# A hand-written planner's DMA costs and the searched order of TensorE's units in a fused attention and feed-forward kernel

## The chip, the cores and the metric

One NeuronCore of one Trainium2 chip. The metric is device microseconds of one execution. Engines are written PE (TensorE), ACT (ScalarE), DVE (VectorE), POOL (GpSimd) and SP (SyncE); PEld is PE's weight load.

## The reference

Attention with "talking heads" (the heads are mixed before and after the softmax), then a feed-forward layer with a squared relu. Eight batches, 12 heads, 448 positions, head size 64, and 2048 hidden units.

```python
scores = scale * q @ k.T                              # [8, 12, 448, 448]
scores = einsum('bhij,hg->bgij', scores, w_pre)       # mix the heads
attn   = exp(scores - max); attn /= sum(attn) + 1e-9
attn   = einsum('bhij,hg->bgij', attn, w_post)        # mix them again
x      = (attn @ v) as [3584, 768]
out    = relu(x @ w_in) ** 2 @ w_out                  # [3584, 768], float32
```

## The kernel before

Matmuls are in bfloat16 and everything runs in one pass over the eight batches, whose stages overlap. Work is recorded as tasks; a task on PE is called a unit. For batches 1 to 7 the way of one batch is:

- **Load.** q, k and v come by DMA from POOL's queue (`load_qk`, `load_v`; L657, L668), the two weights too (`emit_load_w`, L693). DVE makes rounding copies of q and k (`qkr`, L751), PE transposes them (L760), and they are copied to `qkt`.
- **QK** (`emit_QK`, L903). The batch's 448 query rows are cut into four tiles (three of 128 rows, one of 64), written b_T here: 4_3 is tile 3 of batch 4. A unit does two or four heads; ACT or DVE copies each head's scores from PSUM to `stage` (L479 on ACT, L480 on DVE; these two lines serve all copies out of PSUM). `stage` has two slots, used by the tiles in turn.
- **Relayout** (`emit_rel`, L949). The head mix needs 10 query rows x 12 heads on the partitions. SP issues one DMA for every chunk of 10 rows, from `stage` to one of 16 slots of `dring`; chunks that lie across two tiles take two. A batch has 49. All wait for the copies of their tile, and SP issues them in order. The first copy of tile n into `stage` waits until all relayouts of tile n-2 have landed (`old`).
- **Pre-mix** (`emit_pre`, L972). One unit mixes two chunks; ACT takes the exponential and its row sums (`pring`, L989), DVE the reciprocals (L1003), POOL folds them into the weights of the second mix (L1010, L1025).
- **Post-mix** (`emit_post`, L1055 and L1070), which also transposes; its result is copied to `a2t`.
- **AV** (`emit_AV`, L1136) in two halves of a batch, to `xt`.
- **First layer** (`emit_F1`, L1215; L1187 for batches 0 and 1), relu on ACT or DVE (`h1t`), square on DVE (`h2t`).
- **Second layer** (`emit_F2`, L1332; L1281 at the end), copy to `osb`, and the output's DMA from POOL's queue.

Batch 0 does without relayouts for its first 240 rows (L833, L859).

PE's units use its array in five tilings (whole, two halves of rows, four quadrants and others); neighbours in the order may differ in it.

What sets the order is `_Plan`, which runs at build time and whose times never reach the chip. The units stand in ten streams (0 transposes, 1 QK, 2 pre-mix, 3 post-mix, 4 AV, 5 the mix of batch 0's first rows, 6 and 7 first layer, 8 and 9 second layer), and `ORDER` is a string of 947 digits: the next digit names the stream that gives PE's next unit. The string was found by a search against the planner's own times. Between the units `run` places all other tasks: of those that are ready it takes the one that can start first, and a copy or a relu goes to whichever of ACT and DVE would end it first by the planner's costs. So the planner's costs decide where each task stands in its engine's queue and on which engine it runs; on the chip each engine goes through its queue in order and waits on semaphores.

DMAs are of two kinds for the planner, "move" (relayouts) and "load" (all others). `dma_push` notes one when it is issued, with its work in ns; `dma_next` lets both kinds run beside each other at reduced rates and gives the end: the time at which the work is done, and `DMA_END` of its kind on top. SP's queue is held for 1050 ns by each relayout, 850 in batch 0.

Of the kernel before, what the change touches and what calls it, by code (L numbers as in the profile page):

```python
# [21 lines left out]
FETCH = (110e3, 6000.0, 4600.0, 1400.0)  # L22
DMA_START = {"move": 1420.0, "load": 1350.0}
DMA_AHEAD = 3900.0
DMA_END = {"move": 2800.0, "load": 2300.0}
INF = float("inf")
ORDER = (
    "0010000110000111100000000000000005555100511515000015555333555553335555302305155003331254"
    "2211441136332276223766133377223616731226633137114442227663367171613367762227767121623771"
    "3393329122990302183381228324442006627183100281118131813381227673216731326612236773372224"  # L30
    "4411361663177132200663221776338333811282282277006331767332672238001811183118322442293391"
    "3191319222911933392244224431911613362200721731632363732176221673273360021673372281008113"
    "8222891319113933192222443813811381338222444422363163371172261161373372200611637327220062"
    "1637337229300911191139222818323833182222444391139311913392224418223813422813811613622007"
    "3372263362173373262136733702062163711722009139311919222444223811383138111833822281444382"
    "2286116307137062236713733631672127622167337002283812288030911393119311922244422939113933"
    "1913822281183338122444222636371173622267137633363711761263722179228393398128383392224442"
    "2833876383786676767367222676783338444867667766767677679989998888999"
)


# [57 lines left out]
class _Plan:  # L99
# [96 lines left out]

    def dma_push(self, t, start):
        kind, work, packet = t.dma
        at = start + DMA_START[kind]
        if kind == "move" and at < 30e3:  # L200
            at += 600.0
        elif kind == "move" and not self.moving["move"]:
            behind = sum(x[1] for x in self.moving["load"] if x[0] <= at)
            at += min(DMA_AHEAD, max(0.0, behind - max(0.0, at - self.moved)))
        self.moving[kind].append([at, work, packet, t])

    def dma_next(self, go=False):
# [28 lines left out]
        if go:  # L236
            self.moved = now
            for i, y in enumerate((a, b)):
                if y is not None:
                    y[1] = left[i]  # L240
            t = x[3]
            self.moving[t.dma[0]].pop(0)
            t.end = max(t.end, now + DMA_END[t.dma[0]]
                        + (1800.0 if t.dma[0] == "load" and 20e3 < now < 45e3 else 0.0))
# [1251 lines left out]
```

## Time and profile before

| | |
|---|---|
| median of 3 runs | 537.45 us (536.75 to 537.5) |
| the profiled execution | 539.38 us, span 537.6 us |
| mean granted clock of PE | 0.990 |
| busy: PE, ACT, DVE, POOL | 508.3, 436.8, 404.9, 266.3 us |
| DMA | 72.03 MB |
| relayouts in the trace | 365 issues on SP, median 0.905 us each to issue |

Busy time is the time in which an engine has an instruction of its own under way; the rows of an engine's groups give the number of instructions, their mean length and the idle time just before them with what ended it. A granted clock of 1.00 is TensorE's full clock. The profiled execution includes 1.8 us outside the span.

### The profile page before, as it was taken

Reading aid. Unit: us, or ns where it says so; the run is one execution under the profiler, and the core shown is the slowest. Engines: PE = TensorE matmul, PEld = TensorE weight load, DVE = VectorE, ACT = ScalarE, POOL = GpSimd, SP = SyncE. Lnnn points to the kernel's source line nnn. Section 1 sums busy time; section 2 is a strip of 40 time slices with the busy share of each in tenths; the row PEclk is TensorE's granted clock in tenths of the full one; section 3 lists DMA queues with packets and bytes.
Section 4 is the critical chain, followed back from the end, with each engine's and each line's share of the span. In section 5 each row is a group of like instructions: output and inputs, shape, how many; then the busy total and the mean of one; then the engine's idle time right before and its main releaser. Section 6 shows DMA issues by size and latency. Waiting matters only on the chain.

```text
span 537.6 us, 22063 instructions
## 1 busy us (share of the span) xinstructions
PE 508.3 (95%) x8923; PEld 315.1 (59%) x8923; DVE 404.9 (75%) x1057; ACT 436.8 (81%) x1257; POOL 266.3 (50%) x571
## 2 busy tenths in 40 slices
PE   7899999898899996999979999899899999999997
PEld 3355775666666653567535665456545665568874
DVE  8799978688888686877869768887598777965440
ACT  4799999888899895888978999888788888876521
POOL 9926557335763484335733668225735436343100
PEclk9899999999999999999989999999999999999999
DMA  8999999647894689347984579536986668354004
GB/s 112 207 214 182 205 182 180 167 83 136 159 186 96 138 158 190 63 87 151 173 155 102 116 152 203 127 60 134 168 146 119 131 130 160 65 93 104 4 16 104
DMA packets 83065, 72.03 MB, mean 134 GB/s; under 512 B 7572, under 2 KB 80468, under 8 KB 82964
## 3 DMA queue, kind: packets, MB, share of 16 engines
q0 software_dynamic: 37632, 33.83, 39.3%
q1 hardware_dynamic: 45044, 36.59, 29.7%
q8 instruction: 72, 1.18, 0.9%
q14 instruction: 29, 0.24, 0.1%
q10 hardware_dynamic: 288, 0.20, 0.1%
HBM read 47.22 MB, written 11.01 MB: 108 GB/s over the span
## 4 chain that ended last, share of the span: by engine, by line
PE 65%; DMA 13%; ACT 11%; DVE 3%; POOL 3%; SPq 2%; issue 1%; DVEq 0%; ACTq 0%; POOLq 0%
PE ps L1332 22%; PE ps L1215 16%; DMA dring<-stage 8%; ACT pring L989 6%; PE ps L1136 5%; PE ps L972 5%; PE ps L903 4%; PE ps L1055 4%; DMA vraw<-in_v_dram 3%; ACT a2t L479 2%; PE ps L1187 2%; DMA kraw<-in_k_dram 2%; SPq L949 2%; PE ps L1281 2%; DVE stage L480 2%; ACT stage L479 1%
## 5 line engine op out<-in xcount | busy, mean ns | idle before, releaser
L989 ACT ACTIVATE pring<-ps 128x448 bf16<-128x448 f32 x360 | 191.3, 564 | 9.5 <-PE ps L972 8.6
L1332 PE MATMUL ps<-w_out_sb,h2t 64*128 64x384 bf16 x1664 | 151.3, 323 | 0.6 <-DVE a2t L480 0.2
L1010 POOL TENSOR_TENSOR wk2s<-wk2b,rinv 128x120 bf16<-128x120 bf16 (+1 forms) x179 | 70.7, 395 | 162.7 <-DVE rinv L1003 161.5
L480 DVE CAST a2t<-ps 128x420 bf16<-128x420 f32 (+1 forms) x200 | 120.4, 638 | 14.2 <-PE ps L1070 13.5
L480 DVE CAST stage<-ps 128x448 bf16<-128x448 f32 (+1 forms) x182 | 109.3, 616 | 27.3 <-DMA dring<-stage 14.2
L1215 PE MATMUL ps<-xt,w_in_sb 64*128 64x448 bf16 (+2 forms) x1344 | 124.3, 327 | 3.9 <-DVE stage L480 3.6
L479 ACT ACTIVATE stage<-ps 128x448 bf16<-128x448 f32 (+1 forms) x178 | 92.2, 556 | 29.7 <-PE ps L903 15.8
L479 ACT ACTIVATE a2t<-ps 128x420 bf16<-128x420 f32 (+1 forms) x168 | 100.5, 659 | 12.5 <-PE ps L1070 12.3
L1332 PEld LDWEIGHTS ps<-w_out_sb,h2t 64*128 64x128 bf16 x1664 | 76.9, 94 | 51.3 <-issue 2.5
L1215 PEld LDWEIGHTS ps<-xt,w_in_sb 64*128 64x128 bf16 x1344 | 61.7, 95 | 45.1 <-DVE stage L480 3.1
L989 ACT ACTIVATION_READ_ACCUMULATOR pring<-ps 128x1 f32 x360 | 82.5, 229 | 0.0
L1364 POOL DMA_DIRECT2D out_dram<-osb x52 | 33.6, 652 | 90.7 <-ACT pring L989 36.5
L1025 POOL TENSOR_TENSOR ptail<-pring,rinv 128x128 bf16<-128x128 bf16 x171 | 71.3, 417 | 0.0
L972 PE MATMUL ps<-dring,wk 64*64 64x448 bf16 (+1 forms) x672 | 52.7, 365 | 11.7 <-DVE h1t L1244 5.2
L1055 PEld LDWEIGHTS ps<-wk2s,pring 60*128 60x128 bf16 x2160 | 47.3, 94 | 26.4 <-ACT pring L989 3.2
L1244 DVE TENSOR_SCALAR h1t<-ps 128x448 bf16<-128x448 f32 (+2 forms) x93 | 44.2, 478 | 17.3 <-PE ps L1215 12.2
L1055 PE MATMUL ps<-wk2s,pring 60*128 60x60 bf16 x2160 | 55.0, 188 | 2.0 <-ACT a2t L479 1.0
L1253 DVE TENSOR_TENSOR h2t<-h1t 128x448 bf16<-128x448 bf16 (+2 forms) x176 | 53.5, 336 | 1.3 <-ACT h1t L1243 0.8
L903 PE MATMUL ps<-qkt 64*128 64x448 bf16 (+1 forms) x360 | 51.7, 360 | 1.9 <-DVE qkt L480 1.5
L1243 ACT ACTIVATE h1t<-ps 128x448 bf16<-128x448 f32 (+2 forms) x83 | 38.1, 466 | 13.0 <-PE ps L1215 10.9
L1003 DVE RECIPROCAL rinv<-rowsum 128x2 f32<-128x2 f32 (+1 forms) x184 | 28.8, 157 | 25.4 <-ACT pring L989 23.9
L1187 PE MATMUL ps<-xt,w_in_sb 128*128 128x220 bf16 (+1 forms) x384 | 42.4, 260 | 0.5 <-ACT a2t L479 0.4
(66 smaller groups left out, 529.1 us busy)
## 6 DMA issues: line engine op xcount, KB each, us to landing
dring<-stage SPq DMA_DIRECT2D x307, 105.0 KB
out_dram<-osb POOLq DMA_DIRECT2D x52, 192.0 KB, 4.3
vraw<-in_v_dram POOLq DMA_DIRECT2D x48, 128.0 KB, 6.2
qraw<-in_q_dram POOLq DMA_DIRECT2D x48, 112.0 KB, 5.5
kraw<-in_k_dram POOLq DMA_DIRECT2D x48, 112.0 KB, 5.4
w_in_sb<-in_moe_w_in_dram POOLq DMA_DIRECT2D x8, 384.0 KB, 22.2
w_out_sb<-in_moe_w_out_dram POOLq DMA_DIRECT2D x8, 384.0 KB, 18.0
dring<-stage SPq DMA_DIRECT2D x30, 42.0 KB
```

Source lines behind the costliest of these rows:

```text
L479: return eng.activation(o, i_, AF.Copy)
L480: return eng.tensor_copy(o, i_)
L903: r_ = eng.matmul(ps[y * w:(y + 1) * w, g.banks[x], 0:S], qkt[r0:r0 + 64, pb, p + y, 0, i0:i0 + w], qkt[r0:r0 + 64, pb, p + y, 1, :], star ...
L972: r_ = eng.matmul(ps[64 * y:64 * y + 64, gr.banks[x], 0:S], wk1[64 * x:64 * x + 64 - R0 * x, :], dring[64 * x:64 * x + 64 - R0 * x, (g0 + ...
L989: return eng.activation(pring[:, pr, 0:S], ps[:, gr.banks[x], 0:S], AF.Exp, accum_out=rowsum[:, pr, :])
L1010: return eng.tensor_tensor(wk2s[:, p0:p0 + n, :], i0.to_broadcast([128, n, PR]), rinv[:, p0:p0 + n, :].to_broadcast([128, n, PR]), ALU.mult)
L1025: return eng.tensor_tensor(ptail[:, p0 // 2, :, :], pring[:, p0:p0 + 2, 0:PJ], rinv[:, p0:p0 + 2, :].to_broadcast([128, 2, PJ]), ALU.mult)
L1055: r_ = eng.matmul(ps[:, gr.banks[x], o0:o0 + PR], pring[64 * x:64 * x + PR, pr + y, (2 * k + 1) * PJ:(2 * k + 3) * PJ], wk2s[64 * x:64 * x ...
L1187: r_ = eng.matmul(ps[:, g.banks[0], 0:n], w_in_sb[:, ft, t16 * 128:(t16 + 1) * 128], xt[:, ft, c0:c1], start=(ft == 0), stop=(ft == NFT - 1))
L1215: r_ = eng.matmul(ps[:, g.banks[x], 0:n], w_in_sb[64 * y:64 * y + 64, ft, t * 128:(t + 1) * 128], xt[64 * y:64 * y + 64, ft, c0:c1], start ...
L1253: return eng.tensor_tensor(h2t[:, t16, o0:o0 + n], h1t[:, s, 0:n], h1t[:, s, 0:n], ALU.mult)
L1332: r_ = eng.matmul(ps[:, g.banks[hh], 0:FH], h2t[64 * y:64 * y + 64, t16, col:col + 128], w_out_sb[64 * y:64 * y + 64, t16, hh * FH:(hh + 1 ...
```

## The change

Two constants and the string. The planner adds 3700 ns instead of 2800 after a relayout's work, and it takes 4% more time for the work of every other DMA. With these costs the order of PE's units was searched anew, and with it come other places in the queues and other engines for the copies. No task is added or taken away but for PE's warm-up matmuls at the start, which the planner puts in itself; each task does what it did.

```diff
 DMA_AHEAD = 3900.0
-DMA_END = {"move": 2800.0, "load": 2300.0}
+DMA_SLOW = {"move": 1.0, "load": 1.04}
+DMA_END = {"move": 3700.0, "load": 2300.0}
 INF = float("inf")
 ORDER = (
-    "0010000110000111100000000000000005555100511515000015555333555553335555302305155003331254"
+    "0011000011000011100000000000000005550000155001531515551555335553335533255003555001335214"
...
     def dma_push(self, t, start):
         kind, work, packet = t.dma
+        work *= DMA_SLOW[kind]
         at = start + DMA_START[kind]
```

The other ten lines of `ORDER` change as well. The places that the prediction speaks of, as the built programs have them (o a unit of the second layer, h of the first, av of AV; QK by tile):

```text
                         from last QK of 4_0 to first of 4_3     from last QK of 5_0 to first of 5_3
before                   o 6  h 9  av 6  post 15  pre 13         o 11  h 6  av 6  post 17  pre 17
after                    o 8  h 9  av 6  post 17  pre 14         o 11  h 7  av 6  post 19  pre 17
```

Before, POOL issues batch 2's first eight q/k loads ahead of batch 1's last v load; after, the first five.

More of the change, by code (lines that the diff above doesn't have):

```diff
@@ L24 @@
 DMA_AHEAD = 3900.0
-DMA_END = {"move": 2800.0, "load": 2300.0}
+DMA_SLOW = {"move": 1.0, "load": 1.04}
+DMA_END = {"move": 3700.0, "load": 2300.0}
 INF = float("inf")
 ORDER = (
-    "0010000110000111100000000000000005555100511515000015555333555553335555302305155003331254"
[L29 to L38, printed above, removed]
+    "0011000011000011100000000000000005550000155001531515551555335553335533255003555001335214"
+    "2142114123367372262366623331721716233776331167137242244321167611376632137772226632676217"
+    "7333392293093902181238213832444026702181008111813381318312772266622316267117733633262422"
+    "3443317711622676311761300276223833832281383127771266730027622008338111811183324242239119"
+    "3319113922291933392432422443191161136220072371263363362126711773376220063732722008118113"
+    "8221819333911393119224422281833381338222444422163161173372261163733370220611637327220062"
+    "1637337229010911391319222818331831182224422933931393139122442248111812433812286313630027"
+    "3272263363732173621637212763362007317022091391119133922244422181183338111833822281444382"
+    "2286136373227600617117163336372217622673370022882118383009313911193119222444229139131933"
+    "1922283811833382224442226361713736222671376131671373362126721379223938338219938382224442"
+    "2868338367686376736722276776738338444867667767676677679989998898899"
 )
```

## The prediction

> **What bounds the kernel now.** I read the page first, then the chain of waits, then who waited for whom, and last the timeline around the longest waits.
>
> ```profile
> PE 508.3 (95%) x8923; PEld 315.1 (59%) x8923; DVE 404.9 (75%) x1057; ACT 436.8 (81%) x1257; POOL 266.3 (50%) x571
> PE 65%; DMA 13%; ACT 11%; DVE 3%; POOL 3%; SPq 2%; issue 1%; DVEq 0%; ACTq 0%; POOLq 0%
> ```
>
> TensorE (PE) is the bound: busy for 95% of the span. An edit that leaves every instruction alone can win only from the rest, and the chain names the largest other holder, DMA with 13%. In order of time the chain shows where:
>
> ```profile
> 86.09 15.93 DMA vraw<-in_v_dram
> 203.18 8.29 DMA dring<-stage
> 268.72 5.53 DMA dring<-stage
> 330.35 6.68 DMA dring<-stage
> 374.92 6.08 DMA dring<-stage
> 469.74 1.41 PE ps L1332 x16
> 471.34 1.30 PE ps L1332 x16
> ```
>
> Four relayouts (L949) stand in it one by one, some 60 us apart. Who waited for them:
>
> ```profile
> DVE stage L480 <- DMA dring<-stage: 14.2, 7, 4.7
> ACT stage L479 <- DMA dring<-stage: 12.1, 6, 3.9
> ```
>
> It is not the pre-mix (L972) that waits for `dring`, but the copies into `stage`. `stage` has two slots, so the first copy of a tile of scores must wait until the relayouts of the tile before the last have read its slot. It waits at the head of VectorE (DVE) and of ScalarE (ACT), both in order, with the exponentials, relus and `a2t` copies behind it; nothing frees PSUM, and PE stops. The timeline shows each wait with PE's idle time after it:
>
> ```profile
> 211.55 1.27 DVE L480 CAST stage<-ps 64x448 bf16<-64x448 f32 x2 [4.73 <-DMA dring<-stage]
> 213.69 0.63 PE L972 MATMUL ps<-dring,wk 64*64 64x448 bf16 x8 [4.90 <-DVE h1t L1244]
> 274.33 0.63 DVE L480 CAST stage<-ps 64x448 bf16<-64x448 f32 x1 [3.21 <-DMA dring<-stage]
> 275.74 2.42 PE L1215 MATMUL ps<-xt,w_in_sb 64*128 64x448 bf16 x12 [3.01 <-DVE stage L480]
> 278.96 1.31 PE L1215 MATMUL ps<-xt,w_in_sb 64*128 64x448 bf16 x12
> 337.11 0.62 DVE L480 CAST stage<-ps 64x448 bf16<-64x448 f32 x1 [2.37 <-DMA dring<-stage]
> 334.73 0.38 PE L972 MATMUL ps<-dring,wk 64*64 64x448 bf16 x4 [0.65 <-ACT a2t L479]
> 339.09 0.34 PE L1055 MATMUL ps<-wk2s,pring 60*128 60x60 bf16 x12 [1.01 <-ACT a2t L479]
> 339.81 0.38 PE L972 MATMUL ps<-dring,wk 64*64 64x448 bf16 x4 [0.35 <-ACT h1t L1243]
> 381.80 0.57 PE L972 MATMUL ps<-dring,wk 64*64 64x448 bf16 x8 [1.74 <-DVE stage L480]
> ```
>
> By the order of the copies these are tile 3 of batch 3 (211.55, written 3_3 below), 4_3, 5_3 and, at 381, 6_2. A PE stop costs more than its idle time: the unit after the one at 275.74 took 2.42 us where the same twelve matmuls take 1.31, and the granted clock says why.
>
> ```profile
> 213.60:215.00 1.40, 1.31 (x16) 0.67 0.61 170
> 215.00:217.00 2.00, 2.00 (x14) 0.50 1.01 179
> 275.70:277.00 1.30, 1.26 (x8) 0.50 0.53 108
> 379.00:383.00 4.00, 2.26 (x32) 1.00 1.08 156
> ```
>
> The column before the DMA share is the clock: 0.50 after idle of 3.01 and 4.90 us, 1.00 after 1.74. [...]
>
> **The order itself.** The planner's numbers reach the chip only through the order, read from the two built programs. SyncE's queue holds the same relayouts in the same order (one output piece of the last tiles moves; the last unit and what follows it stay). Some 330 copies and relus change between ACT and DVE, but the counts stay (`stage`: 178 and 182 before, 180 and 180 after), so neither engine's load moves. PE's few warm-ups are split differently in the first 16 us, where it waits for loads: nothing. Neighbouring units of unlike array tiling: 284 before, 301 after. A change costs 0.11 us (the two rows of L1332 above, 1.41 with one and 1.30 without), so the 17 cost 1.9 us if nothing covers them. I split the kernel at two points of that order.
>
> Up to the last QK unit of tile 2_0 there are 11 more changes (+1.2), one first-layer unit (L1187, 0.6) and one pre-mix (0.2) fewer: +0.4 us. In this stage PE stops once for a load:
>
> ```profile
> 128.27 0.74 PE L1187 MATMUL ps<-xt,w_in_sb 128*128 128x220 bf16 x6
> 102.16 2.48 PE L1136 MATMUL ps<-a2t,vraw 128*64 128x220 bf16 x60 [1.16 <-DMA vraw<-in_v_dram]
> 30.00:110.00 80.00, 1.00 0.98 185
> ```
>
> After, five of batch 2's q/k loads are issued ahead of batch 1's last v load, not eight. Three of 112 KB at the window's 185 GB/s are an estimate of 1.8 us, more than the 1.16: -1.2 us. The three loads pushed back feed rounding copies (L751) that now stand behind further copies on DVE; if those wait instead, they hold the copies queued behind them: bounds -2.5 to +1.5.
>
> From there to 3_3 the SyncE queue issues without a break:
>
> ```profile
> 115.25 55.17 SPq L949 DMA_DIRECT2D dring<-stage  x49
> 171.09 34.67 SPq L949 DMA_DIRECT2D dring<-stage  x29
> 238.78 33.40 SPq L949 DMA_DIRECT2D dring<-stage  x29
> 298.41 34.87 SPq L949 DMA_DIRECT2D dring<-stage  x29
> ```
>
> 49 issues at 1.13 us, then 29 at 1.20. The planner reckons 1.05 (L949's cost), so it runs ahead of the queue by some 4 us within 29 issues, and the wait at 3_3 ends when this queue has issued so many; after has the same issues. I take 0: the 1.3 us of PE work that after adds here (one unit, one pre-mix, four changes) fall into the wait, and 3_3 is released as before, still with a stop of over 3 us and the slow clock. Bounds: +1.3 if uncovered, -3.4 if PE and not the queue sets this stage (the first QK of 2_2 stands 1.9 us later against 2_0, and the slow clock, 0.33 x 1.4 + 0.50 x 2.0 = 1.5 by the first two clock rows, would go as well).
>
> From 3_3 to the end there are two more changes, and the gain. The price of small units is start to start:
>
> ```profile
> 205.56 0.33 PE L1055 MATMUL ps<-wk2s,pring 60*128 60x60 bf16 x12
> 205.72 0.19 PE L1070 MATMUL ps<-wk2b,ptail 60*128 60x60 bf16 x2
> 205.84 0.38 PE L972 MATMUL ps<-dring,wk 64*64 64x448 bf16 x4
> 206.06 0.36 PE L903 MATMUL ps<-qkt 64*64 64x448 bf16 x4
> ```
>
> 0.28 for a post-mix with its change, 0.22 for a pre-mix.
> - 4_3. Relayouts of 4_0 and 4_1 run back to back (29 in 33.40), so the clock starts at 4_0's last QK. From it to 4_3's first QK, after puts two more second-layer units (2 x 1.30), two post-mixes, one pre-mix and one change: 3.3 us more PE work. The wait of 3.21 is gone, with 3.01 of idle time and 1.1 to 1.3 of slow clock: -4.2. What is late next is PSUM, as in the stretch before it, which lost nothing.
> - 5_3. Between 5_0's last QK and 5_3's first: one more first-layer unit (1.14), two post-mixes, three changes: 1.9 of the idle 0.65 + 1.01 + 0.35: -1.9. Counted from 5_1's last QK it is 1.1, the other bound.
> - 6_2. One more post-mix: -0.2 of 1.74.
> - 3_3 again: after puts its second and third QK side by side, where 6.6 us of work lay between. Their eight copies (0.62 on DVE) take both engines at the release; I charge one: +0.6, bounds 0 and 2.5.
>
> Sum: 0.4 - 1.2 + 0 - 4.2 - 1.9 - 0.2 + 0.6 = -6.5 us. The profiled execution took 539.38 (span 537.6), 1.9 above the median of 537.45, so 532.9 there and 531.0 as median.
>
> **Rivals.**
> (a) The constant is the wrong cure. The four relayouts above, of like size, took 5.53, 6.08, 6.68 and 8.29 us from issue to landing, and the queue's pace is untouched; then a wait shortens only by the 0.9 us that the planner adds. 4_3: 0.9 and the slow clock (1.74 of idle showed none), -2.1; 5_3: -0.9; with the first stage's -0.8 and 3_3's +0.6 that is -3.2: 534.2. [...] For (a) speaks the spread of the four; against it that the order does move 4_3 by 3.3 us, whatever the planner thought.
> (b) PE, not the queue, sets 2_0 to 3_3: -3.4 more, 527.6. Against it: issues without a break.
> (c) Slower: bunched copies. After puts QK units side by side also in 6_2 (four within 2.9 us; before over 12) and 6_3 (second and third; 8.0 apart before). At such a place eight more copies stand before exponentials and relus on both engines: 8 x 0.6 / 2 = 2.4 us, and if PE then idles 3 us, 1.3 of slow clock: 3.7 at each of three places, 11.1 in all, against 7.1 of gains without my charge: 541.4. It decides from 2.4 us a place. For it: ACT is busy 86% in the quiet stretch below; against it: the copies must be done anyway, and where they stood singly before there is now room.
>
> ```profile
> 216.00:256.00 40.00, 39.86 (x754) 24.86 (x750) 30.82 (x78) 34.41 (x101) 17.71 (x40) 0.98 0.49 99
> ```
>
> (d) The orders are alike in effect: what goes at 4_3 and 5_3 comes back at waits that the trace now hides: 537.
>
> **How the numbers follow.** Forecast 0.54, (a) 0.20, (b) 0.08, (c) 0.14, (d) 0.04. The time is the forecast's, 531.0. The range reaches down to (b) with the whole charge at 3_3 gone, 527.0, and up past (a) with the first stage's worse bound (534.2 + 1.5 + 1.2 for the v load that still waits), 537.0; outside lie most of (c) and (d) and a little below. 0.2%, 1.1 us, is what a measurement can tell from no change; the shown runs spread over 0.75. Some of (a) falls within it: faster 0.80, same 0.06, slower 0.14.
>
> **What would show it.** Right: no copy into `stage` at 4_3 waits for `dring` by more than 0.5 us, PE has one stop over 3 us and not two past 100 us, the clock at 4_3 is 1.00, the mean clock rises above 0.990, and the wait for `vraw` is gone. 3_3 must still wait 3 us or more for its relayouts, with 78 issues at 1.13 to 1.20 us ahead of it. Wrong: a wait of 2 us left at 4_3 (a), no stop at 3_3 (b), new PE idle time over 1 us at 6_2 or 6_3 released by ACT or DVE (c).

## The result and the profile after

The new kernel takes 532.52 us in the median (527.3 to 536.3), the kernel before, run beside it, 539.62: ratio 0.987, 95% interval 0.984 to 0.9905. One execution of either kernel took some 1730 us and is left out of the range. The gain is 7.1 us; the forecast was 6.5. The profiled execution took 527.85 us (span 526.0), 11.5 under that of before, more than the medians differ: two more profiles of the new kernel have spans of 527.6 and 527.7, one more of before has 534.9.

Lines of the new kernel stand two further down: its L482 is L480 of before. The page's first row and the chain's shares, after (SPq, PEq and so on are the queues of the engines, which issue):

```profile
PE 506.4 (96%) x8923; PEld 314.1 (60%) x8923; DVE 405.5 (77%) x1066; ACT 436.6 (83%) x1248; POOL 265.3 (50%) x571
PE 67%; DMA 12%; ACT 9%; DVE 7%; SPq 2%; POOL 2%; issue 1%; ACTq 0%; DVEq 0%; POOLq 0%
```

No engine has less to do; PE's share rises because it stops less. DMA still holds 12% of the chain. The chain of waits after has these relayouts between 100 and 300 us. (The chain of before has them there as well: not four in all, as the prediction counted, but also two from 124.38 on, 10.55 us together, and one at 148.29 of 6.98.) The waits for the slots of `stage` are these (total, times, longest):

```profile
141.58 7.16 DMA dring<-stage
196.44 8.51 DMA dring<-stage
259.03 6.11 DMA dring<-stage
...
DVE stage L482 <- DMA dring<-stage: 12.9, 6, 3.3
ACT stage L481 <- DMA dring<-stage: 7.0, 5, 2.8
```

ACT's waits fell from 12.1 to 7.0 us, DVE's hardly (14.2 to 12.9). The timeline around them, as it was read before (the wait at the head of DVE or ACT, and PE's idle time behind it):

```profile
148.82 0.62 DVE L482 CAST stage<-ps 64x448 bf16<-64x448 f32 x1 [2.22 <-DMA dring<-stage]
204.97 0.62 DVE L482 CAST stage<-ps 64x448 bf16<-64x448 f32 x1 [3.31 <-DMA dring<-stage]
206.24 0.38 PE L905 MATMUL ps<-qkt 64*64 64x448 bf16 x4 [2.63 <-DVE h1t L1246]
265.22 2.23 ACT L481 ACTIVATE stage<-ps 64x448 bf16<-64x448 f32 x4 [2.77 <-DMA dring<-stage]
266.94 2.42 PE L1217 MATMUL ps<-xt,w_in_sb 64*128 64x448 bf16 x12 [2.94 <-ACT stage L481]
368.76 0.62 DVE L482 CAST stage<-ps 128x448 bf16<-128x448 f32 x1 [0.81 <-DMA dring<-stage]
416.52 0.62 DVE L482 CAST stage<-ps 128x448 bf16<-128x448 f32 x1 [1.56 <-DMA dring<-stage]
```

At 204.97 (3_3) PE's stop is 2.63 us instead of 4.90. At 265 (4_3) it is 2.94, where it was 3.01, and the unit behind it again takes 2.42 us. In this profile there is no wait at 5_3 and none for `vraw`; at 6_2 the copy waits 0.81, at 7_1 (416.52) 1.56. The granted clock at 3_3 and 4_3 (column before the DMA share):

```profile
206.30:210.00 3.70, 3.27 (x46) 1.47 (x48) 3.61 (x9) 3.12 (x6) 2.18 (x5) 1.00 0.75 203
267.00:268.50 1.50, 1.50 (x10) 0.60 (x12) 1.47 (x4) 1.48 (x4) 0.00 (x0) 0.50 1.10 177
```

The slow clock has gone at 3_3 and stayed at 4_3: the reverse of the forecast.

### The profile page after: what moved, and what is told of

It is laid out like the page before. It is cut to its first block, busy times and chain, and to the rows that moved or that the text cites. A ratio compares the mean times of both kernels' runs of the same rounds, so it can differ in the third digit from the quotient of the medians.

```text
span 526.0 us, 22045 instructions
## 1 busy us (share of the span) xinstructions
PE 506.4 (96%) x8923; PEld 314.1 (60%) x8923; DVE 405.5 (77%) x1066; ACT 436.6 (83%) x1248; POOL 265.3 (50%) x571
## 3 DMA queue, kind: packets, MB, share of 16 engines
q1 hardware_dynamic: 45044, 36.59, 30.2%
## 4 chain that ended last, share of the span: by engine, by line
PE 67%; DMA 12%; ACT 9%; DVE 7%; SPq 2%; POOL 2%; issue 1%; ACTq 0%; DVEq 0%; POOLq 0%
PE ps L1334 21%; PE ps L1217 18%; DMA dring<-stage 10%; PE ps L974 6%; PE ps L1189 5%; PE ps L1138 5%; ACT pring L991 5%; PE ps L1057 5%; PE ps L905 4%; DVE stage L482 3%; PE ps L1283 2%; SPq L951 2%; DMA kraw<-in_k_dram 2%; ACT stage L481 1%; PE ps L762 1%; DVE a2t L482 1%
## 5 line engine op out<-in xcount | busy, mean ns | idle before, releaser
L482 DVE CAST a2t<-ps 128x420 bf16<-128x420 f32 (+1 forms) x201 | 121.2, 639 | 18.2 <-PE ps L1072 17.3
L482 DVE CAST stage<-ps 128x448 bf16<-128x448 f32 (+1 forms) x180 | 107.5, 614 | 24.5 <-DMA dring<-stage 12.9
L481 ACT ACTIVATE stage<-ps 128x448 bf16<-128x448 f32 (+1 forms) x180 | 94.9, 562 | 18.5 <-PE ps L905 10.6
L991 ACT ACTIVATION_READ_ACCUMULATOR pring<-ps 128x1 f32 x360 | 85.4, 237 | 0.0
L1255 DVE TENSOR_TENSOR h2t<-h1t 128x448 bf16<-128x448 bf16 (+2 forms) x176 | 55.0, 340 | 1.4 <-ACT h1t L1245 1.0
L905 PE MATMUL ps<-qkt 64*128 64x448 bf16 (+1 forms) x360 | 50.2, 354 | 5.9 <-DVE h1t L1246 2.6
L974 PE MATMUL ps<-dring,wk 64*64 64x448 bf16 (+1 forms) x672 | 54.0, 365 | 1.9 <-ACT pring L991 1.1
L1138 PEld LDWEIGHTS ps<-a2t,vraw 128*64 128x64 bf16 x960 | 38.8, 109 | 7.0 <-ACT osb L481 2.7
```

Of the source, the lines that this page charges most:

```text
L481: return eng.activation(o, i_, AF.Copy)
L482: return eng.tensor_copy(o, i_)
L905: r_ = eng.matmul(ps[y * w:(y + 1) * w, g.banks[x], 0:S], qkt[r0:r0 + 64, pb, p + y, 0, i0:i0 + w], qkt[r0:r0 + 64, pb, p + y, 1, :], star ...
L974: r_ = eng.matmul(ps[64 * y:64 * y + 64, gr.banks[x], 0:S], wk1[64 * x:64 * x + 64 - R0 * x, :], dring[64 * x:64 * x + 64 - R0 * x, (g0 + ...
L991: return eng.activation(pring[:, pr, 0:S], ps[:, gr.banks[x], 0:S], AF.Exp, accum_out=rowsum[:, pr, :])
L1138: r_ = eng.matmul(po, vraw[:, h, sl, :], m, start=(k == 0), stop=(k == NS))
```

## The experiments

Twelve runs, each profiled and timed beside the kernel before. Three chips were used; the kernel before took 537.2 us (median) beside runs 1 to 4, 541.2 beside 5 to 8 and 538.4 beside 9 to 12, so only ratios, or kernels of one group, are compared. Differences between two kernels of a group are of means, with the 95% interval by their scatter.

To place the time I use one reckoning throughout, called excess: PE's time between two marks (ends of units), less the price of the units between them. The price is the start-to-start time of such a unit in the profile of before, by kind, shape and whether the tiling changes.

**1 and 2. Both kernels again.** No edit.

> The kernel before, once more, for a second profile. Theory W (the time went with waits of the copies into stage for relayouts, which sit at fixed places of the order): the copies of 3_3, 4_3, 5_3 and 6_2 wait again, 4.7, 3.2, 2.4 and 1.9 us in the first profile, each within 1.5 us of that, and PE stops over 2.5 us at 3_3 and 4_3 with the clock at 0.5 behind them. Theory S (scatter: which wait is long is chance from run to run): at least two of the four are under 1 us and others of that length stand elsewhere. Time equal to before, within 0.5%.

> The changed kernel, once more. W: 3_3 waits some 3 us, 4_3 some 2.5 with PE stopped for about 3 us and a slow clock, 5_3 and the wait for v are gone, as in its first profile; 1.3% under before. S: 4_3's wait is gone or another is there. Ratio 0.985 to 0.990 by both.

Before again: 538.89 us, ratio 1.003 (1.000 to 1.007). The new kernel again: 530.91, ratio 0.9895 (0.985 to 0.994). In before's second profile the waits at 3_3 and 4_3 are there and longer, that at 5_3 is 0.85 and that at 6_2 is missing:

```profile
209.71 0.62 DVE L480 CAST stage<-ps 64x448 bf16<-64x448 f32 x1 [6.11 <-DMA dring<-stage]
274.06 0.62 DVE L480 CAST stage<-ps 64x448 bf16<-64x448 f32 x1 [4.65 <-DMA dring<-stage]
```

In the new kernel's second profile 4_3 stops PE again:

```profile
263.59 2.23 ACT L481 ACTIVATE stage<-ps 64x448 bf16<-64x448 f32 x4 [2.08 <-DMA dring<-stage]
265.31 2.41 PE L1217 MATMUL ps<-xt,w_in_sb 64*128 64x448 bf16 x12 [2.26 <-ACT stage L481]
369.81 0.38 PE L974 MATMUL ps<-dring,wk 64*64 64x448 bf16 x4 [2.19 <-DVE stage L482]
```

and 6_2 stops it for 2.19 us, which it did not in the first. So 4_3's stop is fixed to the kernel, and the length of 6_2's changes from run to run. All profiles together show more, since several kernels below have the same string around these tiles. At 5_3 DVE's copy waits in all five profiles with the old string there (0.85 to 3.83 us) and in three of eight with the new one (0.24, 1.28 and 2.23). At 6_2 it is the other way round: with the new string it waits in all eight (0.81 to 3.18 us), with the old one in three of five (1.91, 0.41 and 0.20). Two of these rows, from run 4 (whose lines are numbered as before's) and run 7:

```profile
373.77 0.63 DVE L480 CAST stage<-ps 128x448 bf16<-128x448 f32 x1 [3.18 <-DMA dring<-stage]
377.74 0.62 DVE L482 CAST stage<-ps 128x448 bf16<-128x448 f32 x1 [2.26 <-DMA dring<-stage]
```

**3 and 4. Costs and order apart.**

```diff
 # 3: the new constants, the old string      # 4: the old constants, the new string
-DMA_END = {"move": 2800.0, "load": 2300.0}   DMA_END = {"move": 2800.0, "load": 2300.0}
+DMA_SLOW = {"move": 1.0, "load": 1.04}      -ORDER = (old)
+DMA_END = {"move": 3700.0, "load": 2300.0}  +ORDER = (new)
```

> The order of before with the new constants: PE's units stand as before, 120 copies and relus change their engine, and the loads may shift on POOL. W: the waits at 3_3, 4_3 and 5_3 stay within 1 us, time within 2 us of before. Rival P (the new costs help by where the planner puts the copies and loads): 4 to 7 us faster than before.

> The order of after with the old constants (relayouts 0.9 us earlier for the planner, other DMAs 4% faster); 36 copies change their engine. W: 5 to 8 us faster than before, within 2 us of after. P: within 2 us of before.

The new costs with the old string: 537.63 us, ratio 1.000 (0.9955 to 1.005). The new string with the old costs: 534.82, ratio 0.996 (0.992 to 0.9995). By the means of this chip PE's order alone gives 2.7 us and the new kernel 6.2; the 3.5 between them have an interval of 0.4 to 6.7. The costs alone, which move 120 copies and relus between ACT and DVE and others in their queues, show no gain with an order that was not searched for them. So on this chip the string gave its full gain only with the placement that it was searched with.

**5 to 7. The new string in one stretch, the old one in the others, new costs in all three.**

```diff
 # digits of ORDER      0-239    240-427   428-946
-                       new      new       new
+ # 5: until 2_0        new      old       old
+ # 6: 2_0 to 3_3       old      new       old
+ # 7: from 3_3         old      old       new
```

> New costs; the new order up to the last QK of 2_0 (digits 0 to 239), the old one behind it. The prediction's step: -0.8 us (0.4 of work, -1.2 for the v load): ratio 0.9985. Theory 'moved terms' (from the two profiles: the mark there came 3.0 us earlier, 2.1 of it in the scatter of the first load): about -1, ratio 0.998. Theory 'whole only' (the order pays only as one piece with its costs, since every later queue place was searched on the earlier ones): 0 or slower, 1.000 to 1.010. No wait for vraw in the first two theories.

> New costs; the new order only from the last QK of 2_0 to the first of 3_3 and what stands just behind (digits 240 to 427), the old one before and after. The prediction's step: 0 there and +0.6 for the copies side by side at 3_3: ratio 1.001. Theory 'moved terms': the gain lies here, about -4.6 at 3_3 (shorter wait, PE idle under 3 us, no half clock) and -2.4 before it, ratio 0.987 to 0.992, with the wait at 3_3 down from 4.7-6.1 us to 2-3. 'Whole only': 1.000 to 1.010.

> New costs; the old order up to 3_3, the new one behind it (digits 428 on). The prediction's step: -4.2 at 4_3, -1.9 at 5_3, -0.2 at 6_2, so -6.3: ratio 0.988, with no wait over 0.5 us at 4_3. Theory 'moved terms': 4_3 keeps a wait of 2 us or more and PE's stop of 3 us; 5_3's goes: -1.5 to -3, ratio 0.9945 to 0.997. 'Whole only': 1.000 to 1.010.

| | us | ratio to before | interval |
|---|---|---|---|
| 5, until 2_0 | 537.68 | 0.990 | 0.9835 to 0.996 |
| 6, 2_0 to 3_3 | 536.21 | 0.989 | 0.985 to 0.994 |
| 7, from 3_3 | 535.00 | 0.987 | 0.9815 to 0.992 |
| 8 (below), all three | 531.69 | 0.983 | 0.979 to 0.988 |

None is slower, so "whole only" fell. Each stretch gains; the three lie within each other's intervals, so which gains most is not shown. Runs 5 and 6 gained more than the prediction's steps (0.9985 and 1.001). Run 7 has about the predicted gain (0.988), but not by the predicted mechanism: the wait at 4_3 is there in full.

```profile
270.86 2.23 ACT L481 ACTIVATE stage<-ps 64x448 bf16<-64x448 f32 x4 [3.21 <-DMA dring<-stage]
272.58 2.42 PE L1217 MATMUL ps<-xt,w_in_sb 64*128 64x448 bf16 x12 [3.38 <-ACT stage L481]
```

The three gains add to 3.4%, the whole (run 8, as fast as the new kernel, below) has 1.7%. Part of this is that all three have the new costs; with the old string these gave nothing beside run 3, but that was on another chip, and they were not run alone on this one. I do not take the three ratios as a split of the gain.

**8 to 10. 4_3 later; the new kernel beside it.** Two of 4_3's three QK units go behind six others, three of the first layer, two post-mixes and one pre-mix (the expectation says four). 4_3's first QK unit then comes 40.3 us behind 4_0's last instead of 35.9, so 4.5 later:

```diff
-qk4_3_0 qk4_3_2 h3_0_8_1 post198 h3_0_10_0 post200 pre202 h3_0_10_1
+h3_0_8_1 post198 h3_0_10_0 post200 pre202 h3_0_10_1 qk4_3_0 qk4_3_2
```

> The new kernel with the first two QK units of 4_3 moved behind four first-layer, post-mix and pre-mix units, about 3.3 us of PE's work later. If the wait left at 4_3 (2.5 and 2.8 us on the two engines, PE idle 2.9 us and a slow unit behind) is only lack of work in front of it, it goes with the slow clock: 3 to 4 us faster than the new kernel, ratio to the kernel before 0.981 to 0.984. If it comes back at a later tile (4_3's own relayouts, and with them the chunk shared with batch 4's pre-mixes, are later by as much), it is as the new kernel, 0.987 to 0.990. If the four copies now stand in front of others that PE waits for, slower than the new kernel by 1 to 2 us, 0.990 to 0.993.

> The new kernel unchanged, as the measure for the three beside it: ratio to the kernel before 0.985 to 0.991, mean clock about 0.994, the wait at 4_3 with PE idle 2 to 3 us and a slow unit behind.

> The same edit as in the run late_4_3, now beside the new kernel on one chip. Theory 'lack of work': PE's stop at 4_3 (excess 4.1 to 4.7 us) stays away, with at most 1.4 of it back at 5_2: 2 to 3.5 us under the new kernel, mean clock 0.003 higher. Theory 'given back': within 1 us of the new kernel.

Run 8: 531.69 us, ratio 0.983. Beside each other, run 9 (the new kernel) 532.34, ratio 0.988 (0.982 to 0.993), and run 10 532.45, ratio 0.989 (0.985 to 0.993); difference -0.6 us, interval -4.0 to +2.8. In the timeline of run 10 the copies at 4_3 wait for no relayout, and no PE stop of over 1.0 us is left there:

```profile
271.55 0.52 ACT L481 ACTIVATE stage<-ps 64x448 bf16<-64x448 f32 x1
272.62 1.17 DVE L482 CAST stage<-ps 64x448 bf16<-64x448 f32 x2
273.17 0.58 PE L762 MATMUL ps<-ident,qkr 64*128 64x64 bf16 x28 [1.00 <-ACT pring L991]
```

So the wait at 4_3 is lack of work ahead of the release, and this edit removes it: excess at 4_3 4.7, 4.1 and 4.4 us in three profiles of the new kernel, 2.2 in both with the edit. Yet the time is not shown to fall: the 2.2 us that this would give lie inside the interval, and so does no gain, so run 10 does not decide between its two theories. The two profiles with the edit lose more than this earlier, at 3_3, where the edit has changed nothing: until then all engines have the same instructions in the same queues.

```profile
202.72 0.38 PE L974 MATMUL ps<-dring,wk 64*64 64x448 bf16 x4 [2.23 <-DMA dring<-stage]
207.28 0.62 DVE L482 CAST stage<-ps 64x448 bf16<-64x448 f32 x1 [5.46 <-DMA dring<-stage]
208.55 0.59 PE L905 MATMUL ps<-qkt 64*64 64x448 bf16 x4 [3.07 <-DVE h1t L1246]
```

Excess at 3_3 is 3.2, 2.5 and 2.9 in the new kernel, 6.2 and 6.2 here. What differs is how fast SP gets its relayouts out. First the new kernel, then run 10:

```profile
165.92 34.49 SPq L951 DMA_DIRECT2D dring<-stage  x31
...
166.56 34.23 SPq L951 DMA_DIRECT2D dring<-stage  x29
```

31 issues in the time of 29. Up to the relayout that releases 3_3 the pace is 1.16 to 1.17 us in three profiles of the new kernel, 1.23 to 1.26 in runs 8, 10 and 11, and 1.23 and 1.24 in the two of before. Runs 9 to 11 were on one chip, so it is not the chip. Why the same queue is slower stays open, and that it goes with the kernel and not with the run is not shown. In this stretch run 4, which has the new string, shows 1.25, and runs 3 and 7, which have the old one there, 1.21 and 1.20. In batch 6 the two profiles of before show 1.30 and 1.22. Also, the profiled executions of the new kernel are shorter than most (527.85, 529.48 and 529.70 us; its runs have a mean of 531.9), while those of runs 8 and 10 took 535.67 and 532.47, above the means of theirs (532.1 and 532.0).

**11. 3_3 later as well.**

```diff
-qk3_3_0 pre158 h2_0_8_1 h2_0_6_0 qk3_3_2 qk3_3_4 h2_0_6_1 h2_0_10_0 post154 post156
+pre158 h2_0_8_1 h2_0_6_0 h2_0_6_1 qk3_3_0 h2_0_10_0 post154 post156 qk3_3_2 qk3_3_4
```

> As late_4_3, and 3_3's first QK unit moved behind one pre-mix and three first-layer units (about 3.6 us of PE's work), its other two behind two post-mixes and one first-layer unit more. If at 3_3 too the stop is lack of work before a fixed release of the slot (set by SP's queue), its 2.5 to 6.2 us of excess shrink by 2.5 to 3.6: 2 to 3.5 us under late_4_3. If SP's queue sets the whole stage, so that 3_3's relayouts, now 3 to 4 us later, let it run dry, the same comes back at the pre-mixes of batch 4 or at 4_2 and 4_3: as late_4_3 or up to 2 us over it.

529.33 us, ratio 0.984 (0.978 to 0.9895); against run 10 -2.5 us (-5.0 to -0.1), as "lack of work" had it. The copies at 3_3 wait for nothing in its profile; what is left is a stop at a pre-mix that needs its own relayout, where runs 8 and 10 stopped too, for 2.2 us:

```profile
203.79 0.38 PE L974 MATMUL ps<-dring,wk 64*64 64x448 bf16 x4 [2.74 <-DMA dring<-stage]
204.11 3.82 PE L1217 MATMUL ps<-xt,w_in_sb 64*128 64x448 bf16 x36
208.62 0.63 DVE L482 CAST stage<-ps 64x448 bf16<-64x448 f32 x1
```

Excess from 2_0 to 4_0 is 8.0 us, against 12.4 and 11.3 in runs 8 and 10; 1.5 comes back before 5_0. The mean granted clock of its six runs is 0.998, the highest of all.

**12. The planner's queue made slower.** The hold of SP's queue was raised, and the string searched on from the new one (82 digits differ).

```diff
-                         {SP: (850.0 if b == 0 else 1050.0, 0.0)}, g * 1.0, sem, 16,
+                         {SP: (850.0 if b == 0 else 1110.0, 0.0)}, g * 1.0, sem, 16,
```

> The new kernel with the planner's hold of SP's queue raised from 1050 to 1110 ns a relayout and ORDER searched on for some hours of the planner's time from the new one (82 digits differ; the planner's own gain is 1.5 us at 1110). If the planner's too fast queue is what is left at the waits for the slots, 1 to 3 us under the new kernel. If what is left is what the planner has no term for (half clock behind a stop, the scatter of the landings), no change within 1 us; the stop at 4_3 stays.

528.65 us, ratio 0.981 (0.975 to 0.987). Against the new kernel beside it the difference is -3.7 us with an interval of -7.7 to +0.4, so it is not shown to be faster than it; the same holds for run 11 (-3.1, -6.6 to +0.4). Both beat the kernel before. In its profile 4_3 still waits 2.1 us, and a new wait of 3.0 stands at 4_2; but PE has no stop over 1 us from 5_0 to the end, where two of three profiles of the new kernel have one at 6_2. That the slower queue and not the further search did it is not shown: the two were not run apart.

## Why the prediction was right, and where not

The sum came out (7.1 us for 6.5) from terms that did not. Excess of PE by stretch, two profiles of before and three of the new kernel:

```text
stretch (QK units)       predicted   before       new              excess   work   both
start to last of 2_0       -0.8      7.9   8.5    6.6  5.5  6.3     -2.1    +0.3   -1.8
to first of 4_3            +0.6     14.1  14.3    6.8  6.4  6.0     -7.8    +1.6   -6.2
4_3                        -4.2      4.7   6.8    4.7  4.1  4.4     -1.3     0     -1.3
to first of 6_2            -1.9      3.8   3.4    1.2  1.3  2.3     -2.0     0     -2.0
to the end                 -0.2      3.4   0.6    3.0  6.0  4.0     +2.3    +0.1   +2.4
```

They add to -8.9 (the spans differ by 9.2 in the mean; the medians, over more runs, by 7.1). The profiled executions of the new kernel lie 2.9 us under the mean of its 31 runs, those of before 0.4 under that of its 69, so some 2.5 of the -8.9 belong to the executions that were profiled and not to the change. By runs 8 and 10 the likeliest place for it is the second stretch.

- **First stretch, mis-sized.** The wait for `vraw` went as worked out (-1.2), though not by the string alone: it is gone too in runs 3, 6 and 7, which have the old string there and the new costs. The worse bound, that the loads pushed back would be waited for instead, did not come true; 1.0 more came than was worked out.
- **2_0 to 3_3, "I take 0", wrong for this kernel.** The 1.3 us of added work did fall into waits (+1.4 by the reckoning, -3.1 of excess), and 3_3's stop shrank by 4.4 us more, with its slow clock. I had the queue release 3_3 "as before" since it has the same issues. It has, but its pace is no constant: 1.23 and 1.24 us an issue in before, 1.16 to 1.17 after, over the 26 up to the release 1.6 to 2.0 us. Runs 8 and 10 show that the order is not the whole cause: with the same queues and the slower pace the stretch to 4_3 has 13.3 and 12.2 us of excess, against 14.2 before, and with 1.6 of added work that is my 0. Nor does the pace follow the string: the 26 issues take 30.8 to 32.2 us in the five profiles with the old string there and 30.2 to 32.7 in the eight with the new one. So how much of the -6.2 the change gives is open. Rival (b) had nearly the size (3.4 before 3_3) but not the reason: the queue still sets the release.
- **The +0.6 for copies side by side at 3_3, not seen:** behind the release PE waits 1.3 us (204.97 to 206.24), where it waited 2.1 before. Rival (c)'s places at 6_2 and 6_3 show no stop of their own, only behind late relayouts.
- **4_3, the step that failed.** "The clock starts at 4_0's last QK", so 3.3 us of added work would cover the wait of 3.21. The release itself came later: 36.2 and 37.7 us behind 4_0's last QK in the two profiles of before, 39.1, 38.4 and 38.9 in those of the new kernel, 1.9 in the mean. Some 0.4 of it is SP's first issue; the stream from there to the last issue of 4_1 takes 31.6 to 31.9 us instead of 29.9 and 30.3; from that issue to the release it is 5.5 and 6.7 us before and 6.1, 5.4 and 6.2 after, which adds nothing. So 3.3 us of cover bought 1.4. The row with 29 issues in 33.40 us was right; that the stream would take as long in the new order was an assumption. After, it has 30 in 35.88, 1.20 us each instead of 1.15:

```profile
227.16 35.88 SPq L951 DMA_DIRECT2D dring<-stage  x30
```

  Here the pace does follow the string: to the last issue of 4_1 it takes 29.9 to 30.6 us in the five profiles with the old string there and 30.7 to 32.6 in the eight with the new one; why is open. The added work stands between 4_0 and 4_1, and from 4_1's last QK to 4_3's first it is 21.4 us before and 21.5 after: counted from there, the second bound that I took for 5_3, the gain is nothing, and the truth lies between. Rival (a) gave 0.9 for the wait, and against the first profile it shortened by 0.7 to 1.4 on DVE; but the slow clock stayed, which (a) took to go. PE stopped 1.2 us ahead of the release and then needed ACT's copies, 1.7 us more. Run 10 shows that cover between 4_1 and 4_3 works. Of the 1.1 to 1.3 us of slow clock in this step, which rival (c) uses too, the twelve matmuls show 1.1 (2.42 less 1.31) and no run shows the 1.3: in before the clock is 0.51 over the 3.30 us from 275.70 on, by which I estimate 1.6 (3.30 x 0.49).
- **5_3, right:** -1.9 worked out, -2.0 found, though the wait in before was 2.37 in one profile and 0.85 in the other, and the new kernel's third profile still has one of 1.28.
- **6_2 to the end, mis-signed:** +2.4 instead of -0.2, from waits at 6_2 (0.6, 4.1 and 1.7 us of excess) and one at 7_1 that before did not have. By the eight profiles above the wait at 6_2 goes with the new string and only its length is chance. The prediction took one more post-mix ahead of it for a gain and did not ask when the slot comes free. This is rival (d)'s give-back, at a third of its price.
- **The clock, right in the sum.** Over the runs (one of 1730 us left out), the mean granted clock is 0.988 before (69 runs) and 0.993 after (31). Within either kernel, runs with a clock 0.001 higher are 0.55 to 0.70 us shorter, which makes some 3.0 to 3.8 of the 6.5 us between those means go with fewer slow stretches. That is a correlation, not a run that kept the clock up.

The bound of 0.2% for what can be told apart was too tight: it came from three runs that spread over 0.75 us, while runs of one kernel spread over 9 to 13 us, and with twenty against twenty the interval is 0.7% wide.

## What to carry to other kernels

When work is put in front of a wait, measure the wait from the last event that the release depends on, on both sides, not from the first one of a queue that looks unbroken: here 3.3 us of cover bought 1.4. A queue that runs back to back has a pace, and here the pace moved (1.16 to 1.26 us an issue over the stretch to 3_3); take its spread from several profiles before calling its end fixed. Costs in a planner and the order searched for them are one thing: neither half alone gave the whole gain. And before a table from a few profiles is read as what a change did, compare the profiled executions with the mean of all: here those of the new kernel were 2.9 us under it.

## What the chip showed that was not expected

A stop's length alone does not tell whether the slow clock follows. PE idle for 2.74 us was followed by clock 1.00 in run 11 (204.11 above: 36 matmuls in 3.82 us), 2.63 us by 1.00 in the new kernel; and in run 6 even 3.31 us was followed by 1.00 (the twelve matmuls behind it took 1.31 us). But 2.26 us was followed by 0.51 in the new kernel's second profile, and 2.00 us by 0.53 in run 12, 0.6 us after PE went on. The rows, first run 6, then the second profile, then run 12:

```profile
273.84 1.31 PE L1217 MATMUL ps<-xt,w_in_sb 64*128 64x448 bf16 x12 [3.31 <-DVE stage L482]
273.80:275.20 1.40, 1.35 (x16) 0.55 (x18) 1.35 (x3) 1.35 (x3) 0.00 (x0) 1.00 1.02 150
...
265.30:267.50 2.20, 2.19 (x12) 0.90 (x14) 1.66 (x4) 2.00 (x4) 0.00 (x0) 0.51 0.97 142
...
206.82 0.57 PE L905 MATMUL ps<-qkt 64*64 64x448 bf16 x8 [2.00 <-DVE h1t L1246]
207.40:209.40 2.00, 2.00 (x13) 0.81 (x14) 1.91 (x4) 1.93 (x4) 1.73 (x4) 0.53 0.71 193
```

So stops of 2.00 and 2.26 us were enough for the slow clock, and one of 3.31 us was not; what decides is not shown.

SP's issue of a relayout took from 0.68 to 2.54 us within one stream (171.1 to 205.8 of before), and the mean over the stretch to 3_3 was 1.16 to 1.17 us in three profiles and 1.23 to 1.26 in three others whose queues are the same up to there. Two profiles of one kernel differ nearly as much elsewhere (1.30 and 1.22 in batch 6 of before).
